# A first batch and two weights on their way in: loads reordered, a maximum taken off Pool, a decode planned by single operations

## The chip, the cores and the metric

One core of a Trainium2 chip. Engines: TensorE (PE; its weight loads are PEld), VectorE (DVE), ScalarE (ACT), GpSimd (POOL), and SyncE (SP), which issues all DMAs here. The metric is the device time of one execution in microseconds, the median of the runs shown. TensorE's clock has two levels, 1.2 and 2.4 GHz; the profile gives the granted one as a share of the upper.

## What is computed

Eight batches of Nyström attention (8 heads, 576 tokens, head size 64, 32 landmarks), then a block in which the real part of a 2D FFT is added, normalised, and put through two weight matrices. The weights come in float64, the rest in float32:

```python
A, Bm, C = sm(q, k_lm), sm(q_lm, k_lm), sm(q_lm, k)   # softmaxes, landmarks = means of 18 tokens
Z = Bm.T / (norm(Bm, 1) * norm(Bm, inf) + 1e-6)
for _ in range(6):
    Z = 2 * Z - Z @ Bm @ Z
x = A @ Z @ C @ v
u = x + real(fft(fft(x, axis=1), axis=2))
un = (u - mean(u)) / sqrt(var(u) + 1e-6)
out = u + maximum(un @ w_ch1, 0) @ w_ch2               # 512 -> 2048 -> 512
```

## The kernel before

Python generators emit the program: `attention` (which runs `tokens`, `landmarks` and, through it, `mix` and `norm` of a batch), `weights` and `mlp` are threads, and `run` lets the first of them whose time has come go on to its next `yield`. A model of each engine's time (`now`, `V.free`, `there`) decides when that is, and so the order of the program. TensorE keeps the order in which it is emitted; the other engines' lists are ordered by a scheduler after that. Every engine then executes its own list in order, and SP issues its DMAs in order.

**Weights.** Both matrices come as 16 pieces of 128 x 512 float64, 0.5 MB each, 32 in all. `raw` loads a piece as pairs of 32-bit words (`w_74` in the order lists is the second weight's tile, whose slots hold raw pieces of the first one; others lie in `big` tiles). The float32 bits are put together by integers: ACT takes the absolute value of the high words (`prepare`, into a `row` tile called mag here), Pool raises it to at least `MIN64`, VectorE shifts it left by 3 (the shift, `row<-row`), merges the sign and top bits (`row<-w,row`) and the low word (`w<-w,row`), and ACT takes the piece's maximum (`bound`). When a weight's 16 pieces are there, `scale` finds a power of two for the whole weight, and `halve` splits each piece into two float16 halves (ACT the high, VectorE the low). The split writes in place, one slot further down. `PREP` is how many mags are made ahead, `AHEAD` how many raw pieces beyond that are loaded; six `row` tiles exist.

**First batch.** `load(0)` brings k and q of both head groups (0.58 MB each), then v (0.64 MB each). `tokens` sums landmarks on VectorE (`lm`), takes the maximum of |q| on ACT (`amax`), scales by powers of two (`ab_m`, `ab_d`, `ab_e`), splits q into halves and computes the scores. `landmarks` runs the 6 iterations (`E`, `RE`). `mix` scales by `scw`, splits `Wt` and `Wx`, and makes the tiles `u`; `norm` makes their normalised rows, halves them (ACT the high part, Pool the low by a subtraction) and has SP transpose them into `unT`.

**Two layers.** `mlp` takes two tiles of tokens as a group. The first layer (`h`) needs the group's `unT` and the first weight's split pieces, the second (`acc`) split pieces of the second weight, which exist only after all 32 pieces are decoded.

Of the kernel before, what the change touches and what calls it, by code (L numbers as in the profile page):

```python
# [10 lines left out]
F32 = mybir.dt.float32  # L11
F16 = mybir.dt.float16
I32 = mybir.dt.int32
AF = mybir.ActivationFunctionType
ALU = mybir.AluOpType
# [7 lines left out]
K13 = 2.0**13  # L23
MIN64 = float(np.array([897 << 20], np.int32).view(np.float32)[0])

# [5 lines left out]

AHEAD, PREP = 1, 4

MARGIN, NM, AM, M0 = 1.5, 2.0, 2.0, 0.2

WT = 0.4

# [88 lines left out]
class Kernel:  # L126
    def __init__(self, ctx, tc, NB, q, k, v, w1, w2, t1, t1t, t2, diag, mask, out):
# [17 lines left out]

        self.wraw = []
        self.whole = [self.cp.tile([P, NF + 1, 512], F32, name=f"w{w}") for w in range(2)]
# [18 lines left out]
        self.t1t = const(t1t, [P, 2, 2, 320], F16, "t1t")  # L166
        self.t2 = const(t2, [P, 4, 2, 2, NC], F16, "t2")

    def psum(self):
# [62 lines left out]
    def weights(self):  # L232
# [12 lines left out]
        def prepare(i):  # L245
            while len(self.wraw) < min(2 * NF, i + 1 + AHEAD):
                self.raw()

            mag = self.row(512)
            A.activation(mag, self.wraw[i].rearrange("p (m x) -> p m x", x=2)[:, :, 1].bitcast(F32), AF.Abs)  # L250
            self.G.tensor_scalar(mag, mag, MIN64, None, ALU.max)
            mags.append(mag)

        def bound(i):

            w, f = pieces[i]
            A.activation(mags[i], slots[w][f + 1], AF.Abs, accum_out=am[w][:, f : f + 1])

        es = []

# [13 lines left out]
        for i, (w, f) in enumerate(pieces):  # L274
            while len(mags) < min(2 * NF, i + 1 + PREP):
                prepare(len(mags))
            rv = self.wraw[i].rearrange("p (m x) -> p m x", x=2)
            top, low = rv[:, :, 1], rv[:, :, 0]
            x, dst = mags[i].bitcast(I32), slots[w][f + 1]
            V.tensor_scalar(x, x, 3, 0x3FFFFFFF, ALU.logical_shift_left, ALU.bitwise_and)  # L280
            V.scalar_tensor_tensor(x, top, -0x40000000, x, ALU.bitwise_and, ALU.bitwise_or)
            V.scalar_tensor_tensor(dst.bitcast(I32), low, 29, x, ALU.logical_shift_right, ALU.bitwise_or)
            if i > 0:
                bound(i - 1)
            self.decoded = i + 1
            if self.decoded == 2 * NF:
                self.load(1)
            yield max(0.0, max(self.V.free, self.G.free) - self.now - WT)
            if i == NF:
                yield from scale(0)  # L290
            if es:
                halve()
                yield max(0.0, max(self.V.free, self.G.free) - self.now - WT)
        bound(2 * NF - 1)
# [3 lines left out]
        while sum(self.split_w) < 2 * NF:  # L298
            halve()
            yield max(0.0, max(self.V.free, self.A.free) - self.now - WT)  # L300

    def raw(self):
# [17 lines left out]
        self.wraw.append(raw)  # L320
        self.dma_free = max(self.dma_free, self.now) + 1.5


    def load(self, b):
# [4 lines left out]
        for g in range(2):  # L329
# [3 lines left out]
            nc.sync.dma_start(qf[:, 0 : 16 * SEG].rearrange("p (r t) -> p r t", r=2), self.q[b, :, gs])  # L333
            if b == 0:
                self.raw()
            res.append([kf, qf])
        for g in range(2):
            vf = self.big()
            nc.sync.dma_start(vf.rearrange("p (c d) -> p c d", c=5), self.v[b, g].rearrange("(c p) d -> p c d", p=P))
            res[g].append(vf)  # L340
        self.loads[b] = res
        for t in [res[0][0], res[0][1], res[1][0], res[1][1], res[0][2], res[1][2]]:
            self.dma_free = max(self.dma_free, self.now) + 1.8
            self.there[t.name] = self.dma_free + 2.0

# [592 lines left out]
```

## Time and profile before

| | |
|---|---|
| median of 3 runs | 1074.88 us (1073.45 to 1075.66) |
| the profiled execution's own time | 1075.2 us |
| its span, first to last instruction | 1073.4 us |
| mean granted clock of TensorE | 0.963 |
| busy: PE, PEld, DVE, ACT, POOL | 982.4, 685.5, 621.6, 352.6, 165.6 us |
| moved by DMA | 68.16 MB |

PE's busy time is a model and includes matmuls at the low clock at their full length. Over the whole span PE has 92%; the stages differ, so the rows below are by stage. A DVE or ACT time in a row is that of the instruction, a successor on the same engine starts some 0.07 us before it ends. Rows with a count hold several instructions that ran in a row.

### The profile page before, as it was taken

What the parts mean: (1) busy time and instruction counts of PE and PEld (TensorE: products, weight loads), DVE (VectorE), ACT (ScalarE), POOL (GpSimd) and SP (SyncE); (2) the same over time, 40 slices, a digit from 0 to 9 for tenths busy, and PEclk for the clock granted to TensorE, in tenths of its full rate; (3) what the DMA queues carried; (4) which work ended last, traced back from release to release, by engine and by line L of the source; (5) the groups of instructions that cost most, each with busy time, mean ns of one, the idle gap of its engine ahead of it and who ended that gap; (6) DMA issues with size and microseconds to landing.
All of it is one profiled execution on the core that took longest, in us unless ns stands there. A gap on an engine that the chain in (4) does not pass through costs nothing.

```text
span 1073.4 us, 19661 instructions
## 1 busy us (share of the span) xinstructions
PE 982.4 (92%) x8062; PEld 685.5 (64%) x8062; DVE 621.6 (58%) x1673; ACT 352.6 (33%) x797; POOL 165.6 (15%) x157
## 2 busy tenths in 40 slices
PE   3344588999999999999999999999999999999998
PEld 2233454677776677766776677767776677766665
DVE  6999989768653476446746574567551663441111
ACT  4557656324231333124332332143212332111110
POOL 1763601020101020110202020102010020110000
PEclk9666699999999999999999999999999999999999
DMA  9724502222201130010402031113110000120000
GB/s 331 244 94 162 154 25 90 70 40 86 83 26 26 52 117 21 20 36 16 149 11 49 12 117 43 40 21 121 49 40 20 21 1 21 21 46 15 11 20 20
DMA packets 71018, 68.16 MB, mean 63 GB/s; under 512 B 41360, under 2 KB 59792, under 8 KB 70800
## 3 DMA queue, kind: packets, MB, share of 16 engines
q1 hardware_dynamic: 70928, 66.91, 20.1%
q8 instruction: 63, 1.03, 0.4%
q14 instruction: 27, 0.22, 0.1%
HBM read 48.02 MB, written 9.44 MB: 54 GB/s over the span
## 4 chain that ended last, share of the span: by engine, by line
PE 84%; DVE 10%; ACT 2%; issue 1%; DMA 1%; POOL 1%; SPq 0%; ACTq 0%; POOLq 0%
PE h L196 34%; PE acc L196 34%; PE at L196 15%; DVE w L121 3%; DVE row L121 2%; PE at L201 2%; DVE mid L121 1%; DMA w<-w_dram 1%; DVE big L121 1%; ACT mid L121 1%; ACT row L121 1%; DVE u L121 1%; ACT w L121 0%; DVE lm L121 0%; DVE asum L121 0%
## 5 line engine op out<-in xcount | busy, mean ns | idle before, releaser
L196 PE MATMUL h<-unT,w 128*128 128x256 f16 x3456 | 413.7, 274 | 20.1 <-DMA unT<-row 15.8
L196 PEld LDWEIGHTS <-w 128*128 128x128 f16 x3456 | 337.4, 99 | 90.7 <-DMA unT<-row 16.4
L196 PE MATMUL acc<-w,h 128*128 128x512 f16 x1680 | 395.1, 379 | 0.0
L196 PEld LDWEIGHTS <-h 128*128 128x128 f16 x1680 | 161.8, 98 | 160.8 <-issue 4.1
L121 DVE SCALAR_TENSOR_TENSOR h<-h 128x512 f16<-128x512 f32 x140 | 96.4, 688 | 246.2 <-ACT h L121 245.8
L121 ACT ACTIVATE h<-h 128x512 f16<-128x512 f32 x140 | 83.4, 596 | 357.9 <-PE h L196 357.6
L121 POOL TENSOR_TENSOR r<-ve,mhalf 128x2 f32<-128x2 f32 (+1 forms) x20 | 13.8, 690 | 406.5 <-DVE ve L121 406.4
L121 POOL TENSOR_SCALAR row<-row 128x512 f32<-128x512 f32 x32 | 54.1, 1702 | 58.4 <-ACT row L121 46.9
L121 POOL TENSOR_TENSOR mid<-mid,asum 128x512 f32<-128x512 f32 x14 | 14.8, 1055 | 276.7 <-DVE asum L121 276.7
L196 PEld LDWEIGHTS <-big 128*128 128x128 f16 (+1 forms) x768 | 40.4, 103 | 23.9 <-DVE big L121 9.1
L121 POOL TENSOR_TENSOR row<-row 128x512 f16<-128x512 f32 (+1 forms) x44 | 45.1, 1038 | 36.1 <-ACT row L121 36.1
L196 PEld LDWEIGHTS <-mid 128*128 128x128 f16 x432 | 39.2, 102 | 17.7 <-issue 8.0
L121 ACT CAST row<-row 128x512 f16<-128x512 f32 (+1 forms) x44 | 23.4, 559 | 71.7 <-DVE row L121 69.9
L121 DVE SCALAR_TENSOR_TENSOR row<-at,scw,row 128x262 f32<-128x262 f32 (+1 forms) x48 | 21.3, 486 | 43.7 <-ACT row L121 29.9
L121 DVE TENSOR_REDUCE lm<-big 128x32 f32<-128x576 f32 (+1 forms) x48 | 44.0, 943 | 4.5 <-DMA big<-k_dram 4.1
L121 ACT ACTIVATE row<-w 128x512 f32<-128x512 f32 x54 | 34.4, 642 | 34.6 <-DVE w L121 22.0
L196 PE MATMUL at<-RE,E 128*128 128x96 f32 (+1 forms) x192 | 31.1, 288 | 11.6 <-DVE RE L121 11.6
L196 PEld LDWEIGHTS at<-RE,E 128*128 128x128 f32 x192 | 28.7, 205 | 17.3 <-DVE RE L121 13.3
L121 DVE SCALAR_TENSOR_TENSOR u<-at,scw,row 128x128 f32<-128x128 f32 (+3 forms) x120 | 38.9, 388 | 0.0
L196 PE MATMUL at<-mid,big 128*128 128x262 f16 (+1 forms) x288 | 33.2, 283 | 4.6 <-DVE mid L121 2.3
L121 POOL TENSOR_TENSOR mid<-mid 128x256 f32<-128x256 f32 (+1 forms) x32 | 33.0, 1035 | 21.0 <-ACT mid L121 12.2
L121 DVE SCALAR_TENSOR_TENSOR u<-acc,wsc,u 128x512 f32<-128x512 f32 x36 | 26.8, 746 | 12.0 <-PE acc L196 11.7
(166 smaller groups left out, 998.4 us busy)
## 6 DMA issues: line engine op xcount, KB each, us to landing
w<-w_dram SPq DMA_DIRECT2D x22, 512.0 KB, 4.9
big<-v_dram SPq DMA_DIRECT2D x16, 640.0 KB, 8.3
big<-q_dram SPq DMA_DIRECT2D x16, 584.0 KB, 5.2
big<-k_dram SPq DMA_DIRECT2D x16, 576.0 KB, 4.4
out_dram<-u SPq DMA_DIRECT2D x36, 256.0 KB, 2.0
big<-w_dram SPq DMA_DIRECT2D x10, 512.0 KB, 6.0
unT<-row SPq DMA_TRANSPOSE x72, 2.4
t<-t_dram SPq DMA_DIRECT2D x1, 1048.0 KB, 9.3
```

Of the source, the lines that this page charges most:

```text
L121: return call(out, *args, **kw)
L196: self.nc.tensor.matmul(out, a, b, start=start, stop=stop, skip_group_check=True)
L201: self.nc.tensor.transpose(out, a, ident)
```

## The change

- `load(0)` no longer puts a weight piece behind each pair of k and q: it loads k, q, k, q, then four pieces (`EARLY`), v, four pieces, v. Each DMA's arrival is now part of the model (`arrival`), also that of the constant tables.
- `weights` prepares a piece only when the model has it landed, and waits if the next one to decode has not.
- Pool's maximum is gone. ACT's absolute value gets a scale of 2^-112 in its place, so that the exponent need not be corrected by masking: the shift loses its AND, and the merge takes only the sign bit from the high word.
- After each of the three decode operations the thread yields until the model has VectorE's queue nearly empty (`room`, `WT` 0.1 instead of 0.4), Pool is no longer asked.

```diff
-AHEAD, PREP = 1, 4
+AHEAD, PREP, EARLY = 1, 4, 4
-WT = 0.4
+WT = 0.1
...
         def prepare(i):
-            while len(self.wraw) < min(2 * NF, i + 1 + AHEAD):
-                self.raw()
             mag = self.row(512)
-            A.activation(mag, self.wraw[i].rearrange("p (m x) -> p m x", x=2)[:, :, 1].bitcast(F32), AF.Abs)
-            self.G.tensor_scalar(mag, mag, MIN64, None, ALU.max)
+            A.activation(mag, self.wraw[i].rearrange("p (m x) -> p m x", x=2)[:, :, 1].bitcast(F32), AF.Abs, scale=2.0**-112)
             mags.append(mag)
...
+        room = lambda: max(0.0, self.V.free - self.now - WT)
...
         for i, (w, f) in enumerate(pieces):
             while len(mags) < min(2 * NF, i + 1 + PREP):
-                prepare(len(mags))
+                j = len(mags)
+                while len(self.wraw) < min(2 * NF, j + 1 + AHEAD):
+                    self.raw()
+                if self.raw_there[j] > self.now:
+                    if j > i:
+                        break
+                    yield self.raw_there[j] - self.now
+                    continue
+                prepare(j)
...
-            V.tensor_scalar(x, x, 3, 0x3FFFFFFF, ALU.logical_shift_left, ALU.bitwise_and)
-            V.scalar_tensor_tensor(x, top, -0x40000000, x, ALU.bitwise_and, ALU.bitwise_or)
+            V.tensor_scalar(x, x, 3, None, ALU.logical_shift_left)
+            yield room()
+            V.scalar_tensor_tensor(x, top, -0x80000000, x, ALU.bitwise_and, ALU.bitwise_or)
+            yield room()
             V.scalar_tensor_tensor(dst.bitcast(I32), low, 29, x, ALU.logical_shift_right, ALU.bitwise_or)
...
-            yield max(0.0, max(self.V.free, self.G.free) - self.now - WT)
+            yield room()
...
+    def arrival(self, mb):
+        self.dma_free = max(self.dma_free, self.now) + mb / 0.35
+        return self.dma_free + 1.5
...
             nc.sync.dma_start(qf[:, 0 : 16 * SEG].rearrange("p (r t) -> p r t", r=2), self.q[b, :, gs])
-            if b == 0:
-                self.raw()
...
         for g in range(2):
+            for i in range(EARLY if b == 0 else 0):
+                self.raw()
             vf = self.big()
```

**The order on SP, at the start** (`w_74` is a piece of the first weight, `t` and `t1t` are tables). Before:

```order
L332 DMA big<-k_dram 128x1152
L333 DMA big<-q_dram 128x1168
L311 DMA w_74<-w_dram 128x4x256
L332 DMA big<-k_dram 128x1152
L333 DMA big<-q_dram 128x1168
L311 DMA w_74<-w_dram 128x4x256
L339 DMA big<-v_dram 128x5x256 x2
L143 DMA diag<-ny_dram 128x32
```

With the change:

```order
L348 DMA big<-k_dram 128x1152
L349 DMA big<-q_dram 128x1168
L348 DMA big<-k_dram 128x1152
L349 DMA big<-q_dram 128x1168
L327 DMA w_74<-w_dram 128x4x256 x4
L357 DMA big<-v_dram 128x5x256
L327 DMA w_74<-w_dram 128x4x256 x4
L357 DMA big<-v_dram 128x5x256
L143 DMA diag<-ny_dram 128x32
```

The second k is third instead of fourth, eight pieces stand ahead of the second v instead of two, and diag, which `landmarks` needs, is the fifteenth large or small load after the mask instead of the ninth.

**The order on VectorE in `mix` of the first batch**, around its first two `u` tiles (`w_73<-w_73,wsc` is a split of the first weight, `w_73<-w_74,row` or `w_74<-w_74,row` the last operation of a piece's decode). Before:

```order
L121 SCALAR_TENSOR_TENSOR w_73<-w_73,wsc 128x512
L121 TENSOR_SCALAR row<-row 128x512 x2
L121 SCALAR_TENSOR_TENSOR row<-w_74,row 128x512
L121 SCALAR_TENSOR_TENSOR w_73<-w_73,wsc 128x512
L121 SCALAR_TENSOR_TENSOR w_74<-w_74,row 128x512
L121 SCALAR_TENSOR_TENSOR row<-w_74,row 128x512
L121 SCALAR_TENSOR_TENSOR w_73<-w_73,wsc 128x512
L121 SCALAR_TENSOR_TENSOR row<-at,scw,row 128x262 x2
L121 SCALAR_TENSOR_TENSOR u<-at,scw,row 128x256
L121 SCALAR_TENSOR_TENSOR u<-at,scw,row 128x128 x2
```

With the change:

```order
L121 SCALAR_TENSOR_TENSOR mid<-at,mid 128x262 x2
L121 SCALAR_TENSOR_TENSOR Wx<-at,scw,Wx 32x2x32
L121 SCALAR_TENSOR_TENSOR mid<-at,mid 128x262
L121 SCALAR_TENSOR_TENSOR Wx<-at,scw,Wx 32x2x32 x2
L121 SCALAR_TENSOR_TENSOR row<-at,scw,row 128x262
L121 SCALAR_TENSOR_TENSOR Wx<-at,scw,Wx 32x2x32
L121 SCALAR_TENSOR_TENSOR row<-at,scw,row 128x262
L121 SCALAR_TENSOR_TENSOR Wx<-at,scw,Wx 32x2x32
L121 SCALAR_TENSOR_TENSOR u<-at,scw,row 128x256
L121 SCALAR_TENSOR_TENSOR u<-at,scw,row 128x128 x2
```

Before, decode and splits stand between the links of `mix`, 23 pieces are decoded when the first normalised rows are made; now `mix` stands by itself, and 13 pieces are decoded by then. The splits of the first weight come after it. Up to the 32nd decoded piece both lists hold the same work but for two sums of the second batch.

## Rows read from the trace of the kernel before

**Rows 1.** Busy time of each engine in stretches of 30 us from the start: stretch, its length, then busy us (instructions) of PE, PEld, DVE, ACT, POOL, the granted clock, the DMA engines' share and GB/s.

```profile
0.00:30.00 30.00, 13.04 (x129) 8.70 (x130) 20.36 (x70) 14.92 (x34) 6.97 (x12) 1.00 0.98 333
30.00:60.00 30.00, 9.04 (x85) 7.80 (x83) 29.30 (x59) 14.86 (x36) 21.11 (x14) 0.60 0.54 181
60.00:90.00 30.00, 14.65 (x99) 9.95 (x99) 26.27 (x68) 20.10 (x49) 17.18 (x11) 0.61 0.50 176
90.00:120.00 30.00, 11.89 (x81) 8.58 (x79) 28.68 (x60) 21.35 (x49) 12.85 (x8) 0.65 0.39 111
120.00:150.00 30.00, 24.29 (x197) 20.32 (x196) 28.09 (x54) 18.50 (x38) 10.46 (x8) 0.89 0.34 102
150.00:180.00 30.00, 23.58 (x202) 12.11 (x205) 24.65 (x77) 19.11 (x39) 0.74 (x1) 0.94 0.25 80
```

**Rows 2.** The same view for later stretches.

```profile
300.00:400.00 100.00, 99.42 (x846) 69.65 (x845) 52.56 (x155) 29.00 (x68) 12.98 (x14) 1.00 0.20 59
800.00:1000.00 200.00, 199.42 (x1570) 138.36 (x1568) 80.97 (x221) 44.94 (x98) 17.63 (x19) 1.00 0.08 21
```

**Rows 3.** The timeline of PE: start, us, engine, line, operation, out<-in, tile sizes, count, and in brackets the idle time before it and what ended it.

```profile
42.41 0.42 PE L196 MATMUL at<-kbd,big 128*64 128x64 f16 x4 [9.02 <-DVE big L121]
...
59.13 1.17 PE L196 MATMUL at<-RE,E 128*128 128x96 f32 x4 [3.34 <-DVE RE L121]
...
63.24 1.17 PE L196 MATMUL at<-RE,E 128*128 128x96 f32 x4 [2.94 <-DVE RE L121]
...
113.26 0.39 PE L196 MATMUL h<-unT,w 128*128 128x256 f16 x1 [14.99 <-DMA unT<-row]
```

**Rows 4.** The timeline of VectorE, same columns: the last operation of the last piece's decode.

```profile
144.69 0.68 DVE L121 SCALAR_TENSOR_TENSOR w<-big,row 128x512 int32<-128x512 int32 x1
```

**Rows 5.** The view of the tile row on POOL up to 135 us: count, then ns of one as minimum, median, maximum, first and last start, and shape; then, of those who waited for it, VectorE: us and times.

```profile
L121 POOL TENSOR_SCALAR row<-row x32: 1483/1506/3777, 9.7 to 133.2; 128x512 f32<-128x512 f32 x32
...
  DVE row L121: 1.7, 3
```

**Rows 6.** VectorE's groups of one shape from 0 to 200 us, the decode's three operations: count, then busy us and mean ns of one, then idle time before them.

```profile
L121 DVE TENSOR_SCALAR row<-row 128x512 int32<-128x512 int32 x32 | 16.6, 536 | 1.7 <-POOL row L121 1.7
L121 DVE SCALAR_TENSOR_TENSOR w<-w,row 128x512 int32<-128x512 int32 x22 | 17.7, 811 | 0.0
L121 DVE SCALAR_TENSOR_TENSOR row<-w,row 128x512 int32<-128x512 int32 x22 | 16.3, 751 | 0.0
```

**Rows 7.** The same operations in the view of the tiles row and w up to 180 us, columns as in rows 5.

```profile
L121 DVE TENSOR_SCALAR row<-row x32: 404/420/1369, 11.7 to 142.5; 128x512 int32<-128x512 int32 x32
L121 DVE SCALAR_TENSOR_TENSOR row<-w,row x22: 676/682/1099, 12.2 to 134.4; 128x512 int32<-128x512 int32 x22
L121 DVE SCALAR_TENSOR_TENSOR w<-w,row x22: 643/683/1303, 13.5 to 136.3; 128x512 int32<-128x512 int32 x22
```

**Rows 8.** The timeline of POOL in three stretches, columns as in rows 3.

```profile
34.54 3.10 POOL L121 TENSOR_SCALAR row<-row 128x512 f32<-128x512 f32 x2 [1.07 <-ACT row L121]
...
108.24 1.15 POOL L121 TENSOR_TENSOR row<-row 128x512 f16<-128x512 f32 x1
...
125.36 2.44 POOL L121 TENSOR_TENSOR row<-row 128x512 f16<-128x512 f32 x2
```

**Rows 9.** The timeline of VectorE, partly in the same stretches.

```profile
33.99 1.70 DVE L121 SCALAR_TENSOR_TENSOR row<-w,row 128x512 int32<-128x512 int32 x2
35.62 1.69 DVE L121 SCALAR_TENSOR_TENSOR w<-w,row 128x512 int32<-128x512 int32 x2
...
61.69 1.30 DVE L121 SCALAR_TENSOR_TENSOR w<-w,row 128x512 int32<-128x512 int32 x1
...
108.30 1.37 DVE L121 TENSOR_SCALAR row<-row 128x512 int32<-128x512 int32 x1 [0.37 <-POOL row L121]
...
110.43 1.53 DVE L121 SCALAR_TENSOR_TENSOR w<-big,row 128x512 int32<-128x512 int32 x1
...
125.42 1.37 DVE L121 TENSOR_SCALAR row<-row 128x512 int32<-128x512 int32 x1 [0.72 <-POOL row L121]
```

**Rows 10.** The timeline of VectorE at the start.

```profile
10.42 1.35 DVE L121 TENSOR_REDUCE lm<-big 128x64 f32<-128x1152 f32 x1 [1.50 <-DMA big<-k_dram]
...
21.38 0.27 DVE L121 TENSOR_REDUCE ab_m<-at 4x1 f32<-4x128 f32 x1
```

**Rows 11.** The timeline of ACT at the start.

```profile
9.00 0.66 ACT L121 ACTIVATE row<-w 128x512 f32<-128x512 f32 x1 [7.00 <-DMA w<-w_dram]
...
13.44 0.68 ACT L121 ACTIVATE row<-w 128x512 f32<-128x512 f32 x1 [3.79 <-DMA w<-w_dram]
```

**Rows 12.** The timeline of VectorE around `mix` and `norm` of the first batch: its scale, and the normalised rows of the first and the second pair of tiles.

```profile
78.13 0.15 DVE L121 TENSOR_SCALAR scw<-wx_r 128x1 f32<-128x1 f32 x1
...
105.32 1.00 DVE L121 TENSOR_SCALAR row<-u,mv,r 128x512 f32<-128x512 f32 x2
...
122.38 1.00 DVE L121 TENSOR_SCALAR row<-u,mv,r 128x512 f32<-128x512 f32 x2
```

**Rows 13.** The splits of `Wx` on VectorE, as a group of one shape from 0 to 200 us, columns as in rows 6.

```profile
L121 DVE SCALAR_TENSOR_TENSOR Wx<-at,scw,Wx 32x64 f16<-32x64 f32 x8 | 2.2, 279 | 1.6 <-ACT Wx L121 1.5
```

**Rows 14.** The splits of `Wx` on ACT and the squares of `norm`, in the same view.

```profile
L121 ACT ACTIVATE Wx<-at,scw 32x64 f16<-32x64 f32 x8 | 2.4, 303 | 0.5 <-DVE Wx L121 0.4
...
L121 ACT ACTIVATE row<-u,nm 128x512 f32<-128x512 f32 x4 | 2.8, 711 | 0.0
```

More of the change, by code (lines that the diff above doesn't have):

```diff
@@ L23 @@
 K13 = 2.0**13
-MIN64 = float(np.array([897 << 20], np.int32).view(np.float32)[0])
 TCH = 2
@@ L144, in const @@
             return t
-        self.wraw = []
+        self.wraw, self.raw_there = [], []
         self.whole = [self.cp.tile([P, NF + 1, 512], F32, name=f"w{w}") for w in range(2)]
@@ L167, in __init__ @@
         self.t2 = const(t2, [P, 4, 2, 2, NC], F16, "t2")
+        self.arrival(1.7)
     def psum(self):
@@ L292, in weights @@
                 halve()
-                yield max(0.0, max(self.V.free, self.G.free) - self.now - WT)
+                yield room()
         bound(2 * NF - 1)
@@ L320, in raw @@
         self.wraw.append(raw)
-        self.dma_free = max(self.dma_free, self.now) + 1.5
+        self.raw_there.append(self.arrival(0.52))
     def load(self, b):
@@ L333, in load @@
             nc.sync.dma_start(qf[:, 0 : 16 * SEG].rearrange("p (r t) -> p r t", r=2), self.q[b, :, gs])
-            if b == 0:
-                self.raw()
+            for t in (kf, qf):
+                self.there[t.name] = self.arrival(0.59)
             res.append([kf, qf])
         for g in range(2):
+            for i in range(EARLY if b == 0 else 0):
+                self.raw()
             vf = self.big()
             nc.sync.dma_start(vf.rearrange("p (c d) -> p c d", c=5), self.v[b, g].rearrange("(c p) d -> p c d", p=P))
+            self.there[vf.name] = self.arrival(0.66)
             res[g].append(vf)
         self.loads[b] = res
-        for t in [res[0][0], res[0][1], res[1][0], res[1][1], res[0][2], res[1][2]]:
-            self.dma_free = max(self.dma_free, self.now) + 1.8
-            self.there[t.name] = self.dma_free + 2.0
     def tokens(self, b, st):
```

## The prediction

> **What bounds the kernel now.** I read the busy times by stage first [rows 1, 2]. From 300 us on TensorE is occupied almost without a gap at the granted clock of 1.00 (2.4 GHz, the upper of its two levels), with VectorE at half load: what is left there is TensorE's own work, which the change does not touch. Before that it is the other way round. From 30 to 150 us VectorE is busy 26 to 29 of every 30 us, TensorE 9 to 24, at granted clocks of 0.60 to 0.89. So the time can only come from the first 150 us: every microsecond by which that stretch gets shorter moves the saturated rest forward by the same amount.
>
> TensorE's own waits in that stretch show who sets it [rows 3]: 9.0 us for a split of q on VectorE, 15.0 us for the transposed tile of the first group, which VectorE's and ACT's normalisation delivers late. Two things must be complete before TensorE can be fed without pause: the first batch (its normalised tiles feed the first layer), and all 32 weight pieces, since the second layer's scale is the maximum over all of them. The last piece's decode ends at 145.4 us on VectorE. That event [rows 4] is the one I follow.
>
> **The work does not change, only its order.** VectorE's list of instructions up to the 32nd decoded piece holds the same things before and after: the first batch whole, 32 pieces of three operations, the 16 splits of the first weight, seven h evictions; only two sums over q of the second batch stood ahead of it and now stand behind it, where they come back at once. Setting a scale in ACT's absolute value, dropping the AND from the shift, and another sign mask change no instruction's length or count: nothing. The extra pauses between the three decode operations are pauses of the planner, no instructions. So the gain is what VectorE loses today, by being lengthened or by waiting, less what it will lose anew.
>
> **Term 1, the maximum on Pool, -8.3 us.** The 32 Pool operations, 1.5 us each [rows 5], lie beside VectorE's decode. The mean of the decode's forms [rows 6] stands above their median [rows 7]: the shift 536 against 420 ns (32 times, 3.7 us), the two merges 811 against 683 and 751 against 682 (22 times each, 2.8 and 1.5 us): 8.0 us, and about 1 more for the ten pieces read from the big tiles. The excess sits where Pool runs: under two maxima from 34.54 to 37.64 us the merges took 0.83 and 0.85 us each [rows 8, 9]. But some of it lies beside Pool's other work, which stays: the shifts at 108.30 and 125.42 us (0.95 us over each), the merges at 110.43 (0.85) and 61.69 (0.62), 3.4 us [rows 8, 9]. So 5.6 us of the decode's excess goes, and some 2.7 us of the same kind on splits and first-batch operations beside the maxima, an estimate from single instructions 0.3 to 0.4 us over their median. Bounds: 5.6 and, were nothing disturbed any more, 12.
>
> For this contention the Trainium skill (SBUF — State Buffer, section "Who interferes with whom") has an exclusive lock on the port pair that GpSimd and VectorE share, so that the loser blocks fully. The trace does not agree: four merges ran through 3.3 us in which Pool was busy, each only about 0.2 us longer. By that rule the term would be up to 48 us.
>
> **Term 2, waits for Pool, -1.7 us.** VectorE stood idle three times, 1.7 us in all, for a mag row from Pool [rows 5]. The link ACT, Pool, VectorE becomes ACT, VectorE. Bounds 0 and 1.7: the wait might be for ACT instead.
>
> **Term 3, the arrivals, -3.2 us.** At 10.42 us VectorE had waited 1.50 us for the second k, which was queued behind a weight piece [rows 10]. It is now third, and its data come before VectorE is done with the first q. Price: the pieces and v come later. Between the landing of w at 9.00 and at 13.44 us lie three transfers, 1.48 us each [rows 11]. In the new order the sixth piece is the 11th transfer, thus 13.44 + 5 x 1.48 = 20.8 us, and the second v the 14th, 25.3 us, with diag right behind. On ACT the two sums of |q| now stand behind the sixth piece's absolute value, so the transposed amax reaches VectorE at about 25 us where it did at 21.38 [rows 10], and diag is needed there at about the same time. That is 3.6 us later, but six pieces are decoded by then instead of two, 4 x 1.56 = 6.2 us of work (medians of 0.42, 0.68 and 0.68 [rows 7], less the 0.07 us by which each operation starts before the last one ends), and some 0.6 us of other first-batch operations stand ahead of it too: 3.2 us ahead in all. Bounds: 0 if diag or the sixth piece come 3 us later, 4.5 if 1.3 earlier. The tables behind diag are wanted after 45 us, hidden. The weight loads on SP's queue ahead of the first transposes wait at most for the 13th piece, which VectorE decodes before the first normalised rows: no new wait.
>
> **Term 4, the first batch without filler, +9 us.** Here the change takes something away. From the scale scw at 78.13 us to the normalised rows at 105.32 us VectorE now has 7 pieces and 7 splits between the links of a chain [rows 12], afterwards 2 pieces. The chain itself: ten splits into Wt and Wx, each ACT 0.30 then VectorE 0.28 [rows 13, 14], with four others between, an estimate of 7.5 us; then, estimated in the same way from single instructions, products and u 3.8, two sums and two squares of 0.71 [rows 14] with pieces between on ACT 4.2, Pool's power and the rows 2.5: 18 us, in which VectorE has about 10.5 us to do. The second pair of tiles takes about 13 us for 8.4 of work (its rows wait for buffers that Pool frees), the third tile with the first weight's scale 9.5 for 7.6. Idle in all 14 us, where VectorE today has 3.7 from 60 to 90 us and 1.3 from 90 to 120 [rows 1]. The score chain before it is covered: six products at an estimated 2.3 us (1.17 for the four matmuls, the rest VectorE's copy and the way there and back; 4.1 now with pieces between [rows 3]) against 20.8 us of other VectorE work. Bounds: 0 if the planner's filling holds, +14 if this stretch, 78.2 to 123.4 us today [rows 12], stays 45 us long.
>
> **Sum.** -8.3 - 1.7 - 3.2 + 9 = -4.2 us. The profiled execution took 1075.2 us (span 1073.4), 0.3 above the median of 1074.88; 1075.2 - 4.2 = 1071.0, as a median 1070.7.
>
> **Rivals.** *The cover holds.* Pieces one operation at a time fill the chain's gaps, and term 4 is nearly nothing: -13 us, with the lengthening beside Pool's other work also smaller -19: 1056 to 1066. For it: VectorE was idle only 0.7 us of 30 to 60 us with such filling [rows 1]. Against: in the new order ten splits in a row have no piece between them. *It comes out even*, within 0.2% (2.15 us, about what this measurement can tell from no change): term 4 at 11 to 15 us. *Slower: the first batch's chain becomes the bound.* VectorE executes in order; a link that is late holds every piece behind it. If the mix keeps its 45 us (+5 on my sum) and the score chain keeps the 4.1 us a step at the low clock that it shows now [rows 3], 6 x 1.8 = 11 us more of which 3 are covered, the end is 1070.7 + 13 = 1084. It decides from 4.2 us of idle beyond my term 4, and shows from 6.4. For it: TensorE's granted clock was 0.60 in that stretch [rows 1], and nothing there will raise it. Against: most of today's step length is pieces in the queue, which move away. *The change doesn't do what it says:* the decode is lengthened by something other than Pool's maximum; then terms 1 and 2 vanish and the end is 1081; the merges that were stretched under Pool's maximum [rows 8, 9], beside medians of 0.42 and 0.68 us [rows 7], speak against it. *The full lock* described above would give 1074.9 - 48 - 1.7 - 3.2 + 9, about 1031; the rows all but exclude it.
>
> **How the numbers follow.** Forecast (1066 to 1072.7) 0.50; cover holds 0.16; even 0.15; slower by the chain 0.14; not Pool's maximum 0.03; full lock 0.02. Faster by over 0.2% is 0.50 + 0.16 + 0.02 = 0.68, same 0.15, slower 0.14 + 0.03 = 0.17. The time is that of the forecast. The range goes from 1060, within the cover's case, to 1078, which takes in the even case and the nearer half of the slower ones; about 0.08 lies below and 0.11 above. Faster alone would be 1060 to 1072.7.
>
> **What would show it.** In the changed profile: the decode's shift and merges at means near 0.42 and 0.68 us but for a few beside Pool's subtractions (term 1); no VectorE idle named after a Pool row ahead of a shift (term 2); six pieces decoded before the transposed amax at about 25 us (term 3); scw at about 60 us, the first normalised rows near 78, more idle on VectorE between 60 and 100 us than today (term 4); the last piece decoded at 139 to 142 us; from 200 us on nothing different. I am wrong if the last decode comes at the same time or later, or if it comes earlier and TensorE then waits longer after it.

## Result: 0.6% slower

The changed kernel takes 1081.84 us (median of 4 runs, 1079.11 to 1082.17) against 1074.70 for the kernel before in the same comparison: ratio 1.0061, 95% interval 1.0048 to 1.0073. Forecast were 1070.7 us and a range of 1060 to 1078. The profiled execution is the shortest of the four, 1079.1 us with a span of 1077.3, 3.9 us over the span of before.

**The profile after, by stage.** The view of [rows 1] for the changed kernel, and three short stretches of it:

```profile
0.00:30.00 30.00, 6.09 (x30) 3.42 (x31) 20.98 (x59) 13.24 (x32) 2.06 (x8) 0.82 0.99 335
30.00:60.00 30.00, 18.33 (x207) 14.43 (x207) 26.72 (x73) 15.37 (x36) 4.56 (x5) 0.67 0.40 124
60.00:90.00 30.00, 14.94 (x106) 10.64 (x107) 21.79 (x58) 15.47 (x41) 3.42 (x3) 0.67 0.42 152
90.00:120.00 30.00, 13.75 (x82) 9.41 (x81) 28.10 (x65) 23.24 (x52) 3.41 (x3) 0.59 0.56 171
120.00:150.00 30.00, 19.55 (x157) 14.47 (x158) 29.87 (x56) 21.48 (x43) 0.00 (x0) 1.00 0.38 121
150.00:180.00 30.00, 23.90 (x201) 12.00 (x203) 24.52 (x81) 18.19 (x37) 1.05 (x1) 0.94 0.31 102
...
185.00:190.00 5.00, 2.11 (x12) 0.95 (x10) 5.00 (x11) 2.06 (x5) 2.76 (x4) 0.98 0.02 5
190.00:195.00 5.00, 4.92 (x25) 3.16 (x26) 2.68 (x7) 1.71 (x4) 1.15 (x1) 0.68 0.00 0
195.00:200.00 5.00, 5.00 (x55) 3.97 (x53) 2.95 (x7) 1.86 (x5) 0.00 (x0) 1.00 0.00 0
```

Pool's load is gone, and VectorE is less busy from 30 to 90 us: 26.72 and 21.79 us instead of 29.30 and 26.27. That would be a gain if the work were done earlier. The events say where it went (VectorE's timeline: the transposed amax, `scw`, the normalised rows of the first and second pair, the last decode):

```profile
27.39 0.27 DVE L121 TENSOR_REDUCE ab_m<-at 4x1 f32<-4x128 f32 x1
...
69.03 0.15 DVE L121 TENSOR_SCALAR scw<-wx_r 128x1 f32<-128x1 f32 x1
...
85.62 1.00 DVE L121 TENSOR_SCALAR row<-u,mv,r 128x512 f32<-128x512 f32 x2
...
98.49 1.00 DVE L121 TENSOR_SCALAR row<-u,mv,r 128x512 f32<-128x512 f32 x2
...
144.34 0.69 DVE L121 SCALAR_TENSOR_TENSOR w<-big,row 128x512 int32<-128x512 int32 x1
```

Between the amax and `scw` lies the iteration of the first batch, here its first and its last product on TensorE:

```profile
38.70 0.71 PE L197 MATMUL at<-RE,E 128*128 128x96 f32 x4 [0.30 <-DVE RE L121]
...
58.51 1.12 PE L197 MATMUL at<-RE,E 128*128 128x64 f32 x4
```

The amax is 6.0 us later than in [rows 10], `scw` 9.1 and the rows 19.7 and 23.9 us earlier than in [rows 12], and yet the last decode ends at 145.03 where it ended at 145.37 [rows 4]. So up to there the change gained nothing, and the 3.9 us were lost behind it. TensorE's timeline shows where most of them went, in the iteration of the second batch. The same step before:

```profile
185.61 0.58 PE L196 MATMUL at<-RE,E 128*128 128x96 f32 x4
186.02 2.75 PE L196 MATMUL acc<-w,h 128*128 128x512 f16 x12
189.80 0.69 PE L196 MATMUL at<-RE,E 128*128 128x96 f32 x4 [1.03 <-DVE RE L121]
```

And with the change:

```profile
185.80 0.66 PE L197 MATMUL at<-RE,E 128*128 128x96 f32 x4
186.29 0.81 PE L197 MATMUL acc<-w,h 128*128 128x512 f16 x3
190.08 1.17 PE L197 MATMUL at<-RE,E 128*128 128x96 f32 x4 [2.98 <-DVE RE L121]
191.05 2.51 PE L197 MATMUL acc<-w,h 128*128 128x512 f16 x6
193.40 0.58 PE L197 MATMUL at<-RE,E 128*128 128x96 f32 x4
```

Between the second and the third step of the iteration TensorE has three matmuls of the second layer (the thin step, below), then nothing for 2.98 us; in the five microseconds around and behind that gap's end the granted clock is 0.68, and the third step takes 1.17 us, the fourth 0.58 again. Before, twelve such matmuls stood there.

**Where VectorE's time went.** For each kernel I split its time up to the end of the 32nd decoded piece into gaps between instructions, lengthening (each instruction's time over the lower quartile of its kind, summed) and the rest, all from the traces, in us. How the kinds are formed moves a single value by up to 2 us, the differences used below by under 1 us:

| kernel | last decode ends | gaps | lengthening | rest |
|---|---|---|---|---|
| before | 145.4 | 17.1 | 12.9 | 115.4 |
| changed | 145.0 | 22.5 | 6.4 | 116.1 |
| e2, step filled | 145.9 | 23.2 | 6.3 | 116.4 |
| e3, before without the maximum | 133.9 | 15.5 | 4.0 | 114.4 |
| e4, changed with a maximum | 159.0 | 28.3 | 14.6 | 116.1 |
| e6, e3 and the new loads | 140.3 | 21.9 | 3.4 | 115.0 |
| e10, e2 with the old loads | 136.3 | 18.1 | 3.5 | 114.7 |

The change took 6.5 us of lengthening away and added 5.4 us of gaps and 0.7 of rest. The rest grew although two sums over q of the second batch (1.5 us) now stand behind the last decode: VectorE has 68 gaps there instead of 46, and an instruction behind a gap does not start some 0.07 us before its predecessor's end.

### The profile page after: what moved, and what is told of

Read it like the earlier page. It is cut to its first block, busy times and chain, and to the rows that moved or that the text cites. A ratio compares the mean times of both kernels' runs of the same rounds, so it can differ in the third digit from the quotient of the medians.

```text
span 1077.3 us, 19622 instructions
## 1 busy us (share of the span) xinstructions
PE 984.3 (91%) x8062; PEld 683.0 (63%) x8062; DVE 618.3 (57%) x1673; ACT 351.4 (33%) x797; POOL 111.3 (10%) x125
## 3 DMA queue, kind: packets, MB, share of 16 engines
q8 instruction: 63, 1.03, 0.4%
## 4 chain that ended last, share of the span: by engine, by line
PE 83%; DVE 10%; issue 4%; ACT 1%; DMA 1%; POOL 0%; SPq 0%; ACTq 0%; DVEq 0%; POOLq 0%
PE acc L197 34%; PE h L197 33%; PE at L197 14%; DVE row L121 2%; DVE w L121 2%; PE at L202 2%; DVE mid L121 1%; DVE lm L121 1%; DMA big<-q_dram 0%; ACT mid L121 0%; ACT row L121 0%; DVE big L121 0%; DMA w<-w_dram 0%; ACT w L121 0%; DVE u L121 0%
## 5 line engine op out<-in xcount | busy, mean ns | idle before, releaser
L121 POOL TENSOR_TENSOR row<-row 128x512 f16<-128x512 f32 (+1 forms) x44 | 46.0, 1060 | 37.2 <-ACT row L121 37.2
L121 ACT CAST row<-row 128x512 f16<-128x512 f32 (+1 forms) x44 | 23.2, 559 | 78.1 <-DVE row L121 78.1
L121 DVE SCALAR_TENSOR_TENSOR row<-at,scw,row 128x262 f32<-128x262 f32 (+1 forms) x48 | 21.4, 486 | 42.8 <-ACT row L121 28.9
L121 ACT ACTIVATE row<-w 128x512 f32<-128x512 f32 x54 | 33.8, 638 | 18.3 <-DMA w<-w_dram 9.3
L121 ACT ACTIVATE w<-w,wsc 128x512 f16<-128x512 f32 x32 | 23.0, 720 | 18.3 <-DVE w L121 13.8
```

The source lines that it names most:

```text
L121: return call(out, *args, **kw)
```

## Experiments

All were run in four groups, with the kernel before in each (1074.43, 1074.37, 1075.13 and 1074.74 us; e1 to e4, e5 to e8, e9 to e12, e13 to e16). Medians:

| run | us | ratio to before, interval |
|---|---|---|
| e1 changed again | 1081.44 | 1.0065 (1.0052 to 1.0077) |
| e2 changed, step filled | 1077.16 | 1.0026 (1.0017 to 1.0036) |
| e3 before without maximum | 1067.79 | 0.9931 (0.9917 to 0.9945) |
| e4 changed with maximum | 1097.25 | 1.0209 (1.0195 to 1.0223) |
| e5 e3 + pauses | 1071.62 | 0.9978 (0.9968 to 0.9989) |
| e6 e3 + loads | 1071.85 | 0.9982 (0.9974 to 0.9990) |
| e7 changed, no pauses | 1071.40 | 0.9977 (0.9968 to 0.9985) |
| e8 changed, old loads | 1074.55 | 0.9997 (0.9985 to 1.0008) |
| e9 changed, EARLY 2 | 1077.03 | 1.0024 (1.0014 to 1.0033) |
| e10 e8, step filled | 1067.88 | 0.9937 (0.9925 to 0.9950) |
| e11 e7, EARLY 2 | 1068.65 | 0.9945 (0.9932 to 0.9959) |
| e12 e5, step filled | 1068.30 | 0.9939 (0.9926 to 0.9951) |
| e13 e2, diag first | 1075.75 | 1.0004 (0.9995 to 1.0013) |
| e14 e2, EARLY 0 | 1069.96 | 0.9956 (0.9941 to 0.9972) |
| e15 e7, old loads | 1071.55 | 0.9968 (0.9955 to 0.9981) |
| e16 e8, filled more | 1068.09 | 0.9935 (0.9921 to 0.9949) |

**The thin step: e1, e2.** e1 has no edit.

> The changed kernel once more, nothing edited, as the base of the others and to see whether its loss sits in one place. Theory A (the last decode stands still because the idle time of VectorE grew by what Pool's maximum gave back; the loss comes later, from one step of the second batch's landmark iteration in which TensorE has three matmuls to fill instead of twelve): last decode again at 145 us, a TensorE gap of about 3 us near 187 us, its granted clock near 0.7 from 190 to 195 us, the whole 0.5 to 0.75% above the kernel before. Rival B (the loss is a matter of one execution): gap and low clock are gone from this trace, or sit elsewhere.

It sits in one place: last decode 146.15 us, gap 2.97 us, clock 0.52 from 190 to 195 and 0.80 from 195 to 200 us, span 1079.6. The low clock lasted longer than in the first trace, and the third step of the iteration came 0.8 us later (190.85 us instead of 190.08): the two spans differ by 2.3 us.

```diff
# e2, last loop of weights
-            yield max(0.0, max(self.V.free, self.A.free) - self.now - WT)
+            yield max(0.0, max(self.V.free, self.A.free) - self.now)
```

> The changed kernel with one number: the pause between two splits of the second weight, after all pieces are decoded, waits until VectorE and ACT are modelled empty (0 instead of 0.1 us ahead). Up to the last decode every engine's list is as in the changed kernel; behind it TensorE's list becomes that of the kernel before, with twelve matmuls of the second layer between the second and the third iteration step where the changed kernel has three. Theory A: last decode still at 145 us, the 3 us gap near 187 us shrinks to about 1, the granted clock stays 1.00 from 190 to 195 us, and the time falls by 3.5 us (2.5 to 5) against the changed kernel, to about 0.1 to 0.3% above the kernel before. Rival (the loss comes from the first batch's early place, so it is there before 150 us): no change, still 0.6% above.

4.3 us less, as expected. TensorE's timeline of e2 in the same place:

```profile
186.97 0.58 PE L197 MATMUL at<-RE,E 128*128 128x96 f32 x4
187.38 2.75 PE L197 MATMUL acc<-w,h 128*128 128x512 f16 x12
191.16 0.69 PE L197 MATMUL at<-RE,E 128*128 128x96 f32 x4 [1.03 <-DVE RE L121]
```

And its busy times behind the gap, columns as in [rows 1]:

```profile
190.00:195.00 5.00, 3.97 (x39) 3.51 (x38) 3.06 (x8) 1.25 (x4) 1.79 (x2) 1.00 0.00 2
```

The gap is 1.03 us as in the kernel before, and the clock stays at 1.00. The last decode is where it was (145.9), so this loss is apart from the rest: 2.7 us above the kernel before remain. TensorE's list differs from e1's not in this step alone but from there to some 325 us. The second step starts no earlier in e2 than in e1 (186.97 and 186.57 us); where the two lists are the same again, the same matmul starts at 323.9 in e2 and 328.7 in e1. Gap, low clock and the other order are one price here; no run parts them.

**Pool's maximum: e3, e4.**

```diff
# e3, on the kernel before
-            A.activation(mag, ..., AF.Abs)
-            self.G.tensor_scalar(mag, mag, MIN64, None, ALU.max)
+            A.activation(mag, ..., AF.Abs, scale=2.0**-112)
+            self.G.charge(mag)
...
```

`charge` adds the operation's time to the planner's model of Pool and issues nothing; shift and merge are as in the change.

> The kernel before with only Pool's maximum taken out (ACT's absolute value has the scale, shift and merge as in the change), its time still charged in the planner's model, so that TensorE's and SP's lists are those of the kernel before, VectorE's but for neighbours. Theory A (the contention was real, and the cover of the first batch's chain was lost by the new order, not by a faster decode): the 8.5 us of lengthening beside the maximum and 1.7 us of waits go, the subtractions' part stays at 4 to 6 us, idle time grows by at most 2: last decode at 136 to 139 us, time 7 us below the kernel before (5 to 9), about 1067.7. Rival C (VectorE in this stretch is not bound by its own work; whatever is given back turns into waits for loads and for the first batch's chain): last decode at 142 to 145 us and the time 0 to 2 us below. Were the lengthening not from Pool's maximum at all, it would be the same as before within 1 us.

1067.79, near the number expected; the last decode comes even earlier, at 133.9. The decode's forms in e3, for [rows 6]:

```profile
L127 DVE SCALAR_TENSOR_TENSOR w<-w,row 128x512 int32<-128x512 int32 x22 | 15.8, 716 | 0.0
L127 DVE SCALAR_TENSOR_TENSOR row<-w,row 128x512 int32<-128x512 int32 x22 | 15.4, 703 | 0.0
L127 DVE TENSOR_SCALAR row<-row 128x512 int32<-128x512 int32 x32 | 13.0, 418 | 0.0
```

Means 418, 703 and 716 ns instead of 536, 751 and 811, and the wait of 1.7 us for Pool is gone. Of 11.4 us at the last decode 7.1 arrive at the end of the span, in part because TensorE is behind by then:

```profile
106.27 4.91 PE L202 MATMUL h<-unT,w 128*128 128x256 f16 x24 [13.37 <-DMA unT<-row]
...
120.80 17.41 PE L202 MATMUL h<-unT,w 128*128 128x256 f16 x144 [2.83 <-DVE mid L127]
138.04 0.27 PE L207 MATMUL at<-ident,wm 128*1 128x128 f32 x1
```

The transpose of the second weight's maximum (`wm`) stands behind 144 matmuls of the first layer in TensorE's list. VectorE has `wm` ready at 135.6 us, and the transpose starts at 138.04, 9.9 us earlier than in the kernel before (147.95). So 1.5 us are lost there; where the other 2.8 go was not followed. The first `h` starts 7.0 us earlier than in [rows 3]; that this is also near the gain at the end does not show that it sets it.

```diff
# e4, on the changed kernel
             A.activation(mag, ..., AF.Abs, scale=2.0**-112)
+            self.nc.gpsimd.tensor_scalar(mag, mag, 0.0, None, ALU.max)
```

> The changed kernel with an operation on Pool put back behind ACT's absolute value (a maximum with 0, which changes nothing in the values), not charged in the model: TensorE's list is that of the changed kernel. Theory A (it costs what it cost before, less what falls into VectorE's idle time between 30 and 105 us, 14 us in the changed kernel): 6 to 8 us of lengthening come back beside it, last decode at 149 to 153 us, time 4 to 8 us above the changed kernel. Rival C (the first batch's chain bounds the stretch): under 2 us above. A third way, the link through Pool now late for the decode because pieces are prepared closer to their use: 10 us above or more.

15.8 us more than e1, the third way. The decode's forms:

```profile
L121 DVE TENSOR_SCALAR row<-row 128x512 int32<-128x512 int32 x32 | 19.8, 630 | 5.5 <-POOL row L251 5.5
L121 DVE SCALAR_TENSOR_TENSOR row<-w,row 128x512 int32<-128x512 int32 x22 | 17.1, 783 | 0.1
L121 DVE SCALAR_TENSOR_TENSOR w<-w,row 128x512 int32<-128x512 int32 x22 | 15.2, 700 | 0.0
```

The lengthening that comes back is 8.3 us (14.6 - 6.3), what e3 took away is 8.9: two measurements of the same price. The gaps grow by 4.8 us against e1 (23.5 there), above all by waits for the link through Pool (5.5 us ahead of the shift, where [rows 5] had 1.7); the last decode is 12.9 us later than in e1, and some 3 more are lost behind it.

**Pauses or loads: e5 to e8.** e5 is e3's kernel (planner's charge for Pool dropped too, as in e6) with the two `yield`s and WT 0.1; e6 has the change's `load`, `raw` and `arrival` instead (so what e5 and e6 cost over e3 holds the dropped charge too, which no run has alone); e7 is the changed kernel without the two `yield`s, e8 with the old `load` order:

```diff
# e5
             V.tensor_scalar(x, x, 3, None, ALU.logical_shift_left)
+            yield max(0.0, self.V.free - self.now - WT)
             V.scalar_tensor_tensor(x, top, ...)
+            yield max(0.0, self.V.free - self.now - WT)
# e7
-            yield room()
             V.scalar_tensor_tensor(x, top, ...)
-            yield room()
# e8
+            if b == 0:
+                self.raw()
             res.append([kf, qf])
         for g in range(2):
-            for i in range(EARLY if b == 0 else 0):
-                self.raw()
```

> The kernel before without Pool's maximum (and without its charge in the model), its loads as before, plus the change's two pauses between the three decode operations and its WT of 0.1. In VectorE's list the normalised rows of the first batch now stand at 20 and 22 pieces with none and one split ahead of them (23 and 27 pieces with 7 and 11 splits in the run without the maximum alone), and TensorE has three matmuls between the second and third iteration step of the second batch. Theory A (the pauses between the decode's operations are what takes the filler out of the first batch's chain and thins TensorE's filler later): VectorE idle from 45 to 105 us at 10 to 13 us instead of 5.5, last decode at 139 to 142 us instead of 133.9, the 3 us gap with the low clock behind it, time 8 to 11 us above the run without the maximum alone: 1076 to 1079. Rival L (the order of the loads does it): within 3 us of it, 1066 to 1071.

> The kernel before without Pool's maximum (and its charge), plus the change's order of loads and its model of arrivals alone; no pauses between the decode's operations, WT 0.4, pieces prepared as before. VectorE's list has seven pieces ahead of the transposed amax instead of two, and the same filler later (rows at 22 and 27 pieces, 7 and 11 splits). Theory A (the load order does nearly nothing: what it saves ahead of the amax comes back as a wait behind it): idle to 45 us within 1.5 us of the 8.1 in the run without the maximum alone, last decode at 133 to 136 us, time 1066 to 1070. The forecast's own term of -3.2 us would give 1064.6 and a last decode at 131. Rival L (the loads cost the 6 us of idle that the changed kernel has more): 1073 or more.

> The changed kernel without the two pauses between the decode's three operations; loads, arrivals and WT 0.1 as changed. Rows of the first batch at 19 and 23 pieces with 1 and 7 splits ahead; TensorE's list behind the last decode has the twelve matmuls in the iteration step. Theory A: idle from 45 to 105 us at 6 to 9 us, last decode at 137 to 141 us, no low clock at 190 us, time 1069 to 1074, thus 8 to 12 us under the changed kernel. Rival L (loads): 1077 or more, and what falls is only the 4 us of the later step.

> The changed kernel with the order of loads of the kernel before (a piece behind each pair of k and q, the arrivals still in the model). Two pieces ahead of the amax, 7 at scw, rows at 13 and 15 pieces and no split, TensorE's thin step as in the changed kernel. Theory A (the loads are not what costs): last decode at 143 to 148 us, time 1078 to 1084. Rival L: last decode under 141 us and 1074 or less.

Theory A fell here: it held for e7 (1071.40, last decode 138.9) but not for the others. The loads alone cost 4.1 us on e3 (e6: last decode 140.3, with 5.6 us of gaps from 105 to 120 us alone), and with the old loads the changed kernel is 6.9 us faster (e8: last decode 138.3, although its step is thin, gap 2.98 us). The pauses alone cost 3.8 us (e5), not 8 to 11, and e5 has the thin step too (gap 2.97, clock 0.71 from 180 to 185 us).

**What the pauses cost without the thin step: e10, e12, e16.** e10 is e8 with e2's line; e12 is e5, and e16 is e8, with 0.8 in the place of WT in that line.

> The changed kernel with the old order of loads (1074.6) and also the later pause of 0, so that TensorE has twelve matmuls in the thin step. If the two causes add: 4.3 us below the one with the old loads alone, 1069 to 1071.5, granted clock 1.00 around 185 us. If the step's loss is covered by something else once the loads are back: 1073 to 1075.

> The kernel before without the maximum, with the change's two pauses and WT 0.1, old loads (1071.6), and the later pause 0.8 us ahead, so that TensorE has twelve matmuls of the second layer and six of the first between the second and the third iteration step. If the thin step is what is left of the pauses' cost: 3 to 5 us less, 1066.5 to 1068.5, as fast as without the maximum alone; its last decode stays at 137.5 us, its first transposed tile at 99 us. If the 4 us of idle that the pauses leave at 90 to 105 us count: 1070 or more.

> The changed kernel with the old order of loads and the later pause 0.8 us ahead (twelve matmuls of the second layer and six of the first between the second and third step, instead of twelve). If the 1.03 us gap that is left there counts at the end: 1066 to 1067.5, under 1067.9; if other waits between 150 and 170 us (a split that TensorE waits for) take it back: 1067.5 to 1069.

e10 gains 6.7 us, more than expected, e12 3.3; both end within 0.5 us of e3. So with the old loads the pauses, the arrival model and the wait for landed pieces cost nothing at the end once the step is filled. They do leave gaps: the last decode is 2.4 us later in e10 and 3.2 in e12 than in e3, but TensorE, which gets its first transposed tile 4.4 and 7.5 us earlier than there (101.9 and 98.8 us), has less of its first layer left by then: the transpose of `wm` starts at 137.7 us in e10 and 138.6 in e12, at 138.0 in e3. Filling more (e16) gives nothing further in the median; its trace has a granted clock of 0.66 from 180 to 185 us, which e10's has not.

**Which part of the loads: e9, e11, e13, e14.** e9 is the changed kernel with EARLY 2, e11 also without the pauses, e14 is e2 with EARLY 0, and e13 is e2 with `self.diag32 = const(diag, ...)` moved up behind the mask.

> The changed kernel with two pieces instead of four ahead of each v (EARLY 2); TensorE keeps its thin step of three matmuls. Two pieces instead of six are decoded ahead of the transposed amax, and diag is the eleventh load behind the mask instead of the fifteenth. Theory A2 (the loads cost because the pieces' absolute values stand ahead of ACT's sums of |q|, so that the first batch's chain starts 6 to 7 us late): amax at 21 to 24 us instead of 28, last decode at 138 to 143 us, time 1073 to 1077, near the changed kernel with the old loads (1074.6). Rival V (it is where the second k or v stand): amax may come earlier, but the time stays at 1079 to 1082.

> The changed kernel without the two pauses and with two pieces instead of four ahead of each v. Rows of the first batch at 18 and 21 pieces with 0 and 4 splits. By theory A2 the chain starts 5 to 6 us earlier than in the run without the pauses (1071.4): amax at 21 to 24, last decode at 133 to 137, time 1066 to 1069. Rival (behind the first transposed tile TensorE's own first-layer matmuls are the bound by then, as in the run without the maximum alone): 1069 to 1071.

> The changed kernel with the later pause of 0 (1077.2), and diag loaded right behind the mask instead of fifteenth; TensorE's list is the same, on VectorE one small product moves up. Theory A2 (the chain is late because of ACT's sums of |q|, diag only stands beside): amax still at 27 to 28 us, first RE at 33 to 36, time within 1.5 us of 1077.2. Rival D (diag's late landing holds the iteration): RE at 30 us or earlier, 1071 to 1074.

> The changed kernel with the later pause of 0, and no piece ahead of v (EARLY 0): k, q, k, q, v, v, diag, the tables, then the pieces. No piece is decoded ahead of the transposed amax. Theory A2: amax at 16 to 19 us, the chain 9 to 12 us earlier; VectorE idles longer at the start for want of pieces (first decoded piece at about 27 us instead of 18.5), the time 1068 to 1072. Rival V (the second k in third place or v's place costs): 1075 or more. Rival W (the pieces come too late, the decode itself is what is missing): last decode at 143 us or later and 1075 or more, too, but with idle time ahead of 30 us at 14 us or more.

Fewer pieces ahead, earlier amax, shorter time: with 4, 2 and 0 ahead of each v it starts at 27.4, 21.9 and 18.3 us. e9 is 4.4 us faster than e1, at the upper edge of what was expected (its median 1077.03, last decode 141.0), e11 2.8 us faster than e7 (last decode 136.8), and e14 7.2 us faster than e2; diag's place gives 1.4 (e13, its amax still at 27.7). The amax and the first pair's rows on VectorE in e14, and ACT's sums of |q| in the changed kernel and in e14:

```profile
18.31 0.27 DVE L121 TENSOR_REDUCE ab_m<-at 4x1 f32<-4x128 f32 x1
...
75.42 1.00 DVE L121 TENSOR_SCALAR row<-u,mv,r 128x512 f32<-128x512 f32 x2
```

```profile
23.86 1.16 ACT L121 ACTIVATE big<-big 128x1168 f16<-128x1168 f32 x1
...
25.02 1.16 ACT L121 ACTIVATE big<-big 128x1168 f16<-128x1168 f32 x1
```

```profile
6.71 1.18 ACT L121 ACTIVATE big<-big 128x1168 f16<-128x1168 f32 x1 [4.70 <-DMA big<-q_dram]
...
9.64 1.18 ACT L121 ACTIVATE big<-big 128x1168 f16<-128x1168 f32 x1 [1.65 <-DMA big<-q_dram]
```

Both q had landed by 9.9 us in the changed kernel: ACT's list had six pieces' absolute values and three of their maxima ahead of the sums. From amax to the first rows it is 58.2 us in the changed kernel with 7 pieces between, 57.1 in e14 with 11, 57.7 in e10 with 11:

```profile
19.82 0.27 DVE L121 TENSOR_REDUCE ab_m<-at 4x1 f32<-4x128 f32 x1
...
77.52 1.00 DVE L121 TENSOR_SCALAR row<-u,mv,r 128x512 f32<-128x512 f32 x2
```

So in the lists with pauses this chain's length hardly depends on whether 7 or 11 pieces are its filler (work that stands between its links). A late start is then paid in full: at the first rows 13 pieces are decoded in e2 as in e10, and the six ahead of the amax are missing inside the chain. Of the 9.6 us by which e2's last decode is later than e10's, 5.1 are gaps, 2.8 lengthening and 1.7 rest. With more filler the chain is longer (77.5 us in e3, with 21 pieces and 7 splits), and there a late start need not cost. Why the first stretch then still leaves e14 2.1 us above e10 I did not separate; nor did I follow why e15 misses:

> The changed kernel with the old order of loads and without the two pauses: what is left of the change is Pool's maximum gone, the arrivals in the model and the wait for a piece that has not landed. Its lists have the twelve matmuls in the iteration step. Expected as without the maximum alone: 1066.5 to 1069; if model and wait cost something by themselves, 1070 or more.

1071.55 instead of 1066.5 to 1069: 4.2 us of gaps from 90 to 105 us, last decode 138.8. Without the pauses this kernel is 3.7 us slower than e10; the reason is open. Beside e7 the run shows something else. Amax and first rows in e7, then in e15:

```profile
28.41 0.28 DVE L121 TENSOR_REDUCE ab_m<-at 4x1 f32<-4x128 f32 x1 [0.82 <-PE at L202]
...
92.17 1.00 DVE L121 TENSOR_SCALAR row<-u,mv,r 128x512 f32<-128x512 f32 x2
```

```profile
20.26 0.27 DVE L121 TENSOR_REDUCE ab_m<-at 4x1 f32<-4x128 f32 x1
...
85.22 0.99 DVE L121 TENSOR_SCALAR row<-u,mv,r 128x512 f32<-128x512 f32 x2
```

By their edits the two differ only in the loads. The amax is 8.1 us later with the new ones, the first rows 6.9 us, and yet the last decode (138.9 and 138.8 us) and the time (1071.40 and 1071.55; 0.9977 and 0.9968 of the kernel before in their groups) are the same within 1 us. So a late start does not cost by itself: it costs together with the pauses.

**One way from before to e1.** Before to e3 -6.6 (maximum), e3 to e10 +0.1 (pauses, arrival model, WT, with the step filled), e10 to e2 +9.3 (loads), e2 to e1 +4.3 (thin step): +7.0. That the steps add up shows nothing, since each starts where the last one ended; and they cross the groups, in which the kernel before differs by up to 0.8 us. The steps are not independent: the loads cost 9.3 us with the pauses and the step filled, 6.9 with the pauses and the thin step (e8 to e1), 4.1 on e3 without the pauses (e6), and at most 1 in the changed kernel without them (e15 to e7). Another way would give the pauses more and the loads less; what is shown is that the two together cost, and that either alone need not (e10; e7 beside e15). e3 and e10, both 0.6 to 0.7% below the kernel before, beat both kernels and cannot be told apart.

## Why the prediction was wrong

- **Bound.** Half right. The last decode led, but it was said that nothing changes from 200 us on and that every microsecond gained up to 150 us arrives. TensorE's order behind the last decode did change, from the thin step on, and there 4.3 us went (e2): the stretch from 150 to 200 us stood in no term. The new order of TensorE's list shows it. And not all of a gain at the last decode arrives (e3: 11.4 us there, 7.1 at the end).
- **Term 1, -8.3:** right as a price: -8.9 in e3, 8.3 in e4; and 8.0 us of the lengthening in the kernel before lie on instructions beside Pool's maximum. In the changed kernel 6.5, for 5.6 us of lengthening now lie beside Pool's other work instead of 4.2 (1.66 us for a merge at 86.99, for one). One reading was off: the four merges of [rows 9] took 0.68, 1.09, 0.68 and 1.09 us, so two were not lengthened and two by 0.41 us, where the mean had each longer by 0.2; and Pool was busy in 2.8 of those 3.3 us.
- **Term 2, -1.7:** right; gaps fell by 1.6 us in e3.
- **Term 3, -3.2:** the step that failed. It counted the six pieces ahead of the amax as gained, as if VectorE's amount of work were the bound, set the amax at 25 us, and had bounds of 0 and -4.5. The arrivals were right (sixth piece at 20.7 us, second v at 25.6), but the amax came at 27.4: the pieces' absolute values ahead of ACT's sums were counted, the three maxima among them were not. Above all, what follows is a chain: with the change's pauses its start is paid in full and the six pieces are missing inside it, so the loads cost +9.3 us (e2 against e10). A loss was never in the bounds, nor that this term and the pauses of term 4 depend on each other (without the pauses the same loads cost at most 1 us, e7 and e15).
- **Term 4, +9:** near in size (+7.4 us of idle time along the chain), but more than half of it in another place. From `scw` on, the chain is as forecast: 16.6 us to the first rows (18) and 12.9 to the second (13). But in the 40.5 us behind `scw` VectorE is idle 6.8 us, not 14 (3.8 before, from 78.1 to 123.4). Between amax and `scw`, which the forecast called covered, it is idle 8.3 us (27.4 to 69.0; 3.9 before, from 21.4 to 78.1). There the six products kept 4.0 us a step and not 2.3. So `scw` came at 69.0 instead of 60: 2.4 us by the amax, 6.6 between. In e10 the products take 4.0 us too and the idle times are 5.3 and 6.0 us, and yet the whole of pauses and plan costs 0.1 us at the end there.
- **Sum at the last decode:** -4.2 forecast, -0.3 measured in the first trace; the end +3.9 to +7.
- **Rivals.** *Slower by the chain* (1084) had the right sign and the right place, with the wrong price: the mix did not keep its 45 us (30 from `scw` to the second pair's rows); the score chain did keep its 4 us a step, the chain started late besides, and a second loss came on top. *Not Pool's maximum* is out by e3 and e4, *the full lock* too.

## To carry to other kernels

A transfer or piece of work that is put ahead of a chain is no gain where the chain is the bound: it delays the chain's start and takes away what would have filled its gaps. Whether the chain is the bound depends on the rest of the order (here the same loads cost 9.3 us with the pauses and at most 1 without), so look first at what each engine's list has ahead of the chain's first link and how much it has between the links. When a planner's constant changes, read the order of every engine to the end of the ramp, not only at the places that the change is about: an order with three matmuls instead of twelve in one step cost as much here as half the contention had. Change what is sure (an operation taken off a shared engine) apart from what moves the plan, and measure them apart.

## What the hardware showed

- VectorE beside Pool's 1.5 us maximum is either not lengthened at all or by up to 0.45 us: of 15 shifts that overlapped one in the kernel before, the first six show 0.01, 0.27, 0.27, 0.27, -0.01 and 0.00 us over the quartile; beside a subtraction it is up to 0.95 us [rows 8, 9], in the changed kernel up to 0.98. The Trainium skill (SBUF — State Buffer, section "Who interferes with whom") has the shared pair locked for the whole instruction; the trace does not agree: a merge that began at 34.60 us, inside a maximum from 34.54 to 36.02, ended at 35.69, and 32 maxima of 48 us in all cost VectorE 8.3 to 8.9 us.
- TensorE's granted clock fell after the gap of 2.97 or 2.98 us in each kernel that had it (0.68 in the first trace of the changed kernel, 0.52 in e1, 0.71 in e5, 0.50 in e8 and e9, in the five microseconds around or behind it) and not after those of 1.02 or 1.03 us (1.00 in e2, e3, e6 and e7). Two shorter gaps in a row went either way: 1.46 and 1.10 us were followed by 0.66 in e16, 1.35 and 1.10 us by 1.00 in e12. The time to come back differed between executions of the same kernel: 1.00 from 195 us in one, 0.80 in the other.
